# Linear attention on one core: the store of head 29 split 5, 121 and 2 and issued by GpSimd and SP, in place of 51, 13 and 64 by SP

## The chip, the core and the metric

The kernel runs on one core of one Trainium2 chip. The metric is the device time of one execution in microseconds (us). Three runs of the kernel before took 169.27, 169.34 and 169.89 us, median 169.34 us.

## What is computed

For each of 32 heads, with q, k and v of 2048 rows by 128 columns in bf16:

```python
phi_q = jnp.where(q > 0, q + 1, jnp.exp(q)) + 1e-6
phi_k = jnp.where(k > 0, k + 1, jnp.exp(k)) + 1e-6
kv = jnp.einsum("bhsd,bhse->bhde", phi_k, v)
z = jnp.einsum("bhsd->bhd", phi_k)
num = jnp.einsum("bhqd,bhde->bhqe", phi_q, kv)
den = jnp.einsum("bhqd,bhd->bhq", phi_q, z)[..., None] + 1e-6
return num / den
```

So each head reads three tensors of 512 KB and writes one of 512 KB: 50.33 MB in, 16.78 MB out.

## The kernel before

A head is one 128-partition tile per tensor: partition p holds 16 consecutive rows, 4096 bytes that are contiguous in the DRAM tensor too (`rows`). k, v and q each have six input buffers (`NBI`), the output `o_sb` has ten (`NBO`), and head h uses output buffer h mod 10. ScalarE takes the exponentials, GpSimd and VectorE make the clamped parts of phi, TensorE transposes q, sums phi_k times v into `kvz_ps` and then the numerators and denominators into `o_ps`, and VectorE (in the last heads ScalarE as well, `div_act`) divides into `o_sb`.

The order of the work is written out by hand. `Plan.add` registers an operation with its engine and a key; every engine, SP too, works its operations off in the order of their keys. `Plan.emit` adds the semaphore waits that the reads and writes call for. A DMA increments the semaphore of its slot by 16 (`dma=("o", slot)`), and a slot's semaphore is one of `dsems`. After its last DMA, SP waits until every slot of the output has its full count (the lines after `if e == "sp"`, line 226 of the profile); then the program ends.

All loads are issued by SP. The key of a store is `late = h + 1.0 + 0.18 * h`, which is later than the key of any load for the heads from 20 on, so the last dozen stores are issued after the last load. Heads 0 to 28 and 30 go out as one DMA of 128 partitions. Head 29 (`LAST - 2`) goes out as three DMAs by the tuple in `PARTS`: partitions 0 to 50, 51 to 63 and 64 to 127, all in slot 9. Head 31 goes out as two, tiles 0 to 8 (2304 bytes a partition) in slot 1 and tiles 9 to 15 (1792 bytes) in slot 10. No later head reuses the output buffer of heads 22 to 31.

GpSimd's own last operation is the addition of line 407 for head 31, with a key of 31.5; the key of the store of head 29 is 35.22.

Of the kernel before, what the change touches and what calls it, by code (L numbers as in the profile page):

```python
# [7 lines left out]
P = 128  # L8
# [241 lines left out]
def bass_standalone__linear_attn_elu__prompt_kernel(  # L250
# [6 lines left out]
    B, H, S, D = q.shape  # L257
    assert D == P and S == 16 * P
    NT = 16
# [3 lines left out]
    NBI = 6  # L263
    NBO = 10
# [2 lines left out]
    NG = 7  # L267
    HALF = NT * P // 2
    LAST = NH - 1
    PARTS = {LAST - 2: (51, 13, 64)}  # L270

    ADD = (1, 2, 3, 4, 5)
    SPLIT = tuple(j for j in range(NT) if j not in ADD)
# [8 lines left out]
    of = out.rearrange("b h s d -> (b h) s d")  # L282

    with ExitStack() as es:
# [28 lines left out]
        def dma_sem(name):  # L313
            return dsems[name]

        for n, c in (("k", NBI), ("q", NBI), ("v", NBI), ("va", 1), ("o", NBO + 1)):
            for i in range(c):
                dsems[(n, i)] = es.enter_context(nc.semaphore(f"s_{n}{i}"))

        block = es.enter_context(nc.Block())  # L320
        pl = Plan()

        def rows(x, h):
            return x[h].rearrange("(p j) d -> p (j d)", j=NT)
# [52 lines left out]
        for h in range(NH):  # L377
# [3 lines left out]
            bi, b2, b3, bo = h % NBI, h % 2, h % 3, h % NBO  # L381
# [201 lines left out]
                last_tile(h + 0.925)  # L583
                div(4, 5, h + 0.93)

            def store(t0, t1, key, parts, slot, p0=0, p1=P, h=h, bo=bo):
                pl.add("sp", key, lambda sp: sp.dma_start(rows(of, h)[p0:p1, t0 * D:t1 * D],
                                                          o_sb[p0:p1, bo, t0:t1].rearrange("p j d -> p (j d)")),
                       reads=[("o", bo, p) for p in parts], dma=("o", slot))

            late = h + 1.0 + 0.18 * h
            if h < LAST:
                p0 = 0
                for n in PARTS.get(h, (P,)):
                    store(0, NT, late, ("t", 0, 1, 2, 3, 4), bo, p0, p0 + n)
                    p0 += n
                assert p0 == P
            else:
                store(0, 9, late, (0, 1, 2), bo)
                store(9, NT, late + 0.01, (3, 4, "t"), NBO)  # L600
# [30 lines left out]
```

## Time and profile before

| | |
|---|---|
| median of three runs | 169.34 us |
| the profiled execution's own time | 169.59 us |
| its span, first to last instruction | 167.78 us |
| TensorE clock granted, mean | 0.991 |
| PE, DVE, ACT, POOL busy | 94%, 92%, 93%, 60% of the span |
| DMA | 67.25 MB, mean 401 GB/s |
| DMA, busy share of its 16 queues, 150 to 158 us | 1.02 to 1.03 (a full queue reads a little over 1) |

How to read it: times in the tables are counted from the first instruction. 1.81 us of the profiled execution lie outside the span. An issue by SP shows as a short instruction on SP's queue; when the data landed is read from the updates of the DMA's semaphore, of which the trace has one for each of the sixteen DMA queues that took part. The trace also has every DMA packet with its start, duration and size, but not the queue's number; since the packets of a busy queue follow each other within 4 ns, the packets can be strung into sixteen chains all the same. The last packet of a queue's share of a DMA is one of 4 bytes, which carries the semaphore's update.

### The profile page before, as it was taken

To read this page: it belongs to the slowest core of one execution; us is meant where nothing else is said; L and a number is where in the kernel's file an instruction comes from. 1 tells how busy PE (TensorE), PEld (TensorE's weight loads), DVE (VectorE), ACT (ScalarE), POOL (GpSimd) and SP (SyncE) were. 2 spreads that over 40 slices of the span, in tenths; PEclk is the share of its full clock that TensorE was granted. 3 is DMA by queue.
4 is the path that set the end of the run, shared out by engine and by line. 5 is a ranking of instruction groups with operands and counts; after the bars stand their busy time and mean duration, and the time that the engine had idled before them with its cause. 6 is when DMAs were issued, how large, how long until landed. Compare 5 with 4: busy or idle time off the path is not lost.

```text
span 167.8 us, 6512 instructions
## 1 busy us (share of the span) xinstructions
PE 158.3 (94%) x3143; PEld 151.3 (90%) x2449; DVE 154.2 (92%) x302; ACT 156.0 (93%) x143; POOL 100.8 (60%) x69
## 2 busy tenths in 40 slices
PE   7579999999999999999999999999999999999960
PEld 0259999999999999999999999999999999999950
DVE  0479999999999999999999999999999999999991
ACT  3969999999999999999999999999999999998790
POOL 2405677666666776666677766666777666666300
PEclk9999999999999999999999999999999999999996
DMA  5999999999999999999999999999999999999975
GB/s 192 367 419 421 413 410 416 413 421 408 414 417 416 419 418 417 421 419 416 414 419 421 415 417 422 416 417 420 418 419 419 420 415 417 421 418 415 410 242 221
DMA packets 19885, 67.25 MB, mean 401 GB/s; under 512 B 2082, under 2 KB 2210, under 8 KB 19874
## 3 DMA queue, kind: packets, MB, share of 16 engines
q1 hardware_dynamic: 19872, 67.12, 99.4%
q8 instruction: 5, 0.08, 0.2%
q14 instruction: 6, 0.05, 0.1%
q10 hardware_dynamic: 2, 0.00, 0.0%
HBM read 50.33 MB, written 16.78 MB: 400 GB/s over the span
## 4 chain that ended last, share of the span: by engine, by line
PE 85%; DVE 5%; DMA 4%; ACT 1%; SPq 1%; issue 0%; DVEq 0%
PE kvz_ps L428 35%; PE o_ps L499 17%; PE o_ps L500 16%; PE xT_ps L452 15%; DMA k_sb<-in_k_dram 4%; DVE o_sb L540 3%; PE kvz_ps L346 1%; ACT ek_sb L396 1%; SPq L389 1%; DVE rden_sb L528 1%; DVE rq_sb L472 0%; DVE emq_sb L484 0%; DVE den_sb L522 0%; DVE emk_sb L402 0%; DVE o_sb L533 0%
## 5 line engine op out<-in xcount | busy, mean ns | idle before, releaser
L407 POOL TENSOR_TENSOR rk_sb<-rk_sb,emk_sb 128x640 bf16<-128x640 bf16 x30 | 41.9, 1397 | 45.8 <-DVE emq_sb L484 44.5
L428 PE MATMUL kvz_ps<-v_sb,rk_sb 128*128 128x128 bf16 (+1 forms) x512 | 68.0, 218 | 0.9 <-DVE rk_sb L407 0.9
L540 DVE TENSOR_TENSOR o_sb<-o_ps,rden_sb 128x768 bf16<-128x768 f32 (+2 forms) x62 | 67.8, 1134 | 0.0
L399 POOL TENSOR_SCALAR rk_sb<-k_sb 128x2048 bf16<-128x2048 bf16 x31 | 58.7, 1895 | 9.5 <-DMA k_sb<-in_k_dram 9.5
L396 ACT ACTIVATE ek_sb<-k_sb 128x2048 bf16<-128x2048 bf16 x32 | 61.5, 1921 | 3.0 <-DMA k_sb<-in_k_dram 2.9
L463 ACT ACTIVATE eq_sb<-xT_ps 128x2048 bf16<-128x2048 bf16 (+1 forms) x33 | 60.1, 1825 | 3.3 <-PE xT_ps L452 2.2
L500 PE MATMUL o_ps<-kvs_sb,rq_sb 128*128 128x129 bf16 (+1 forms) x536 | 61.1, 217 | 0.0
L499 PE MATMUL o_ps<-kvs_sb,emq_sb 128*128 128x129 bf16 (+1 forms) x536 | 61.1, 217 | 0.0
L346 PE MATMUL kvz_ps<-ones_sb,rk_sb 128*128 128x1 bf16 x428 | 58.5, 165 | 0.0
L428 PE MATMUL kvz_ps<-v_sb,emk_sb 128*128 128x128 bf16 (+1 forms) x334 | 53.9, 218 | 0.8 <-DVE emk_sb L402 0.7
L499 PEld LDWEIGHTS o_ps<-kvs_sb,emq_sb 128*128 128x128 bf16 x536 | 50.6, 98 | 0.0
L500 PEld LDWEIGHTS o_ps<-kvs_sb,rq_sb 128*128 128x128 bf16 x536 | 50.1, 97 | 0.0
L428 PEld LDWEIGHTS kvz_ps<-v_sb,rk_sb 128*128 128x128 bf16 x512 | 46.4, 96 | 3.0 <-DVE rk_sb L407 1.8
L346 PE MATMUL kvz_ps<-ones_sb,emk_sb 128*128 128x1 bf16 x253 | 41.5, 165 | 0.0
L452 PE MATMUL xT_ps<-ident,q_sb 128*128 128x128 bf16 x512 | 33.8, 219 | 1.2 <-DMA q_sb<-in_q_dram 0.9
L452 PEld LDWEIGHTS xT_ps<-ident,q_sb 128*128 128x128 bf16 x512 | 29.9, 98 | 5.4 <-DMA q_sb<-in_q_dram 4.4
L428 PEld LDWEIGHTS kvz_ps<-v_sb,emk_sb 128*128 128x128 bf16 x334 | 32.1, 96 | 1.1 <-DVE emk_sb L402 0.8
L470 ACT ACTIVATE rq_sb<-xT_ps 128x1024 bf16<-128x1024 bf16 x30 | 30.5, 1018 | 0.0
L402 DVE TENSOR_SCALAR emk_sb<-ek_sb 128x2048 bf16<-128x2048 bf16 x32 | 21.9, 683 | 5.2 <-ACT ek_sb L396 5.2
L472 DVE TENSOR_SCALAR rq_sb<-xT_ps 128x1024 bf16<-128x1024 bf16 x34 | 23.3, 690 | 0.6 <-ACT eq_sb L463 0.6
L484 DVE TENSOR_SCALAR emq_sb<-eq_sb 128x2048 bf16<-128x2048 bf16 x32 | 22.0, 688 | 0.0
L533 DVE TENSOR_TENSOR o_sb<-o_ps,rden_sb 128x128 bf16<-128x128 f32 x31 | 9.0, 291 | 1.1
(29 smaller groups left out, 52.2 us busy)
## 6 DMA issues: line engine op xcount, KB each, us to landing
k_sb<-in_k_dram SPq DMA_DIRECT2D x32, 512.0 KB, 14.4
q_sb<-in_q_dram SPq DMA_DIRECT2D x32, 512.0 KB, 14.1
v_sb<-in_v_dram SPq DMA_DIRECT2D x32, 512.0 KB, 14.4
out_dram<-o_sb SPq DMA_DIRECT2D x30, 512.0 KB, 15.1
out_dram<-o_sb SPq DMA_DIRECT2D x1, 288.0 KB, 3.2
out_dram<-o_sb SPq DMA_DIRECT2D x1, 256.0 KB
out_dram<-o_sb SPq DMA_DIRECT2D x1, 224.0 KB, 3.1
out_dram<-o_sb SPq DMA_DIRECT2D x1, 204.0 KB
```

What stands on the lines that cost most here:

```text
L346: return pe.add_instruction(mybir.InstMatmult(start_tensor_calc=start, stop_tensor_calc=stop, ldweights=False, bass_skip_group_check=True, ...
L396: lambda a, bi=bi, b2=b2: a.activation(ek_sb[:, b2, :], k_sb[:, bi, :], ACT.Exp),
L399: lambda e, bi=bi, b3=b3: e.tensor_scalar(rk_sb[:, b3, :], k_sb[:, bi, :], BIG, 0.0, op0=ALU.min, op1=ALU.max),
L407: pl.add(eng, key, lambda e: e.tensor_tensor(out=rk_sb[:, b3, c], in0=rk_sb[:, b3, c], in1=emk_sb[:, b3, c], op=ALU.add), reads=[("emk", b ...
L428: last = pe.matmul(kvz_ps[:, 1 - l:NC + r], lhsT=w, rhs=v_sb[:, bi, c - l:c + D + r], start=first, stop=fin, skip_group_check=True)
L452: last = pe.transpose(xT_ps[:, j * P:(j + 1) * P], q_sb[:, bi, j * P:(j + 1) * P], ident[:])
L463: halves[part] = pl.add("act", key, lambda a: a.activation(eq_sb[:, b2, c], xT_ps[:, c], ACT.Exp), reads=both[part:part + 1] or both, writ ...
L470: f = lambda a: a.activation(rq_sb[:, b3, c], xT_ps[:, c], ACT.Relu)
L472: f = lambda d: d.tensor_scalar(rq_sb[:, b3, c], xT_ps[:, c], 0.0, None, op0=ALU.max)
L499: pe.matmul(o_ap, lhsT=emq_sb[:, b3, t * P:(t + 1) * P], rhs=kvs_sb[:, b3, c0:c1], start=True, stop=False)
L500: return pe.matmul(o_ap, lhsT=rq_sb[:, b3, t * P:(t + 1) * P], rhs=kvs_sb[:, b3, c0:c1], start=False, stop=True)
L540: pl.add("dve", key, lambda d: d.tensor_tensor(out=o_sb[:, bo, 3 * g0:3 * g1, :].rearrange("p (a b) d -> p a b d", b=3), in0=_ap(full, bas ...
```

## The change

The tuple for head 29 now names for each part the issuing engine, the slot and the number of partitions: GpSimd issues partitions 0 to 4 in a slot 11 of its own, then partitions 5 to 125 in a slot 12; SP issues partitions 126 and 127 in slot 9. Two semaphores are added. Nothing else differs: the same bytes go to the same places, and all other heads go out as before. The keys of the three parts are the same 35.22 as before, now on GpSimd's list and on SP's.

```diff
-    PARTS = {LAST - 2: (51, 13, 64)}
+    PARTS = {LAST - 2: (("pool", NBO + 1, 5), ("pool", NBO + 2, 121), ("sp", NBO - 1, 2))}
...
-        for n, c in (("k", NBI), ("q", NBI), ("v", NBI), ("va", 1), ("o", NBO + 1)):
+        for n, c in (("k", NBI), ("q", NBI), ("v", NBI), ("va", 1), ("o", NBO + 3)):
...
-            def store(t0, t1, key, parts, slot, p0=0, p1=P, h=h, bo=bo):
-                pl.add("sp", key, lambda sp: sp.dma_start(rows(of, h)[p0:p1, t0 * D:t1 * D],
+            def store(t0, t1, key, parts, slot, p0=0, p1=P, eng="sp", h=h, bo=bo):
+                pl.add(eng, key, lambda e: e.dma_start(rows(of, h)[p0:p1, t0 * D:t1 * D],
                                                           o_sb[p0:p1, bo, t0:t1].rearrange("p j d -> p (j d)")),
...
-                for n in PARTS.get(h, (P,)):
-                    store(0, NT, late, ("t", 0, 1, 2, 3, 4), bo, p0, p0 + n)
+                for eng, slot, n in PARTS.get(h, (("sp", bo, P),)):
+                    store(0, NT, late, ("t", 0, 1, 2, 3, 4), slot, p0, p0 + n, eng)
```

## The prediction, made before the result was known

> **What bounds the kernel now.** I read the last ten microseconds first, in the stretch table by 1 us: columns are the stretch, its length, busy time of PE, PE's weight loads, DVE, ACT and POOL, the granted clock, the DMA's busy share and GB/s.
>
> ```profile
> 162.00:163.00 1.00, 0.40 (x7) 0.22 (x4) 0.93 (x5) 0.86 (x4) 0.00 (x0) 1.00 0.31 107
> 163.00:164.00 1.00, 0.00 (x0) 0.00 (x0) 1.00 (x4) 0.97 (x4) 0.00 (x0) 1.00 0.98 393
> 164.00:165.00 1.00, 0.00 (x0) 0.00 (x0) 0.15 (x1) 0.00 (x0) 0.00 (x0) 0.80 0.92 360
> 165.00:166.00 1.00, 0.00 (x0) 0.00 (x0) 0.00 (x0) 0.00 (x0) 0.00 (x0) 0.50 0.85 328
> 166.00:167.00 1.00, 0.00 (x0) 0.00 (x0) 0.00 (x0) 0.00 (x0) 0.00 (x0) 0.50 0.19 71
> ```
>
> After 164.2 us no engine computes; only DMA is left, and in the last full microsecond just a fifth of its queues. So some queues end later than the rest. SP's waits after 156 us say the same (total, times, longest): line 226 is its closing wait.
>
> ```profile
> SPq L587 <- DVE o_sb L540: 4.5, 1, 4.5
> ...
> SPq L226 <- DMA out_dram<-o_sb: 2.5, 1, 2.5
> ```
>
> Then the issues: the timeline of the last division and of the last store (start, duration).
>
> ```profile
> 163.61 0.55 DVE L540 TENSOR_TENSOR o_sb<-o_ps,rden_sb 128x384 bf16<-128x384 f32 x1
> 164.18 0.33 SPq L587 DMA_DIRECT2D out_dram<-o_sb  x1
> ```
>
> Issued at 164.18, that store lands on its first queue at 166.10, on eleven queues by 166.25, and on the others at 166.63, 166.73, 167.00, 167.14 and **167.30**, the end. The program closes at 167.78, 0.48 us later.
>
> Which queues are those? Landing records of the late stores, in us; "late" are the last five of sixteen:
>
> ```
> head 28 (issued 153.54): 159.43 to 159.89 on 7 queues, 160.75 to 161.74 on 8, then 163.99
> head 30 (issued 162.13): 164.65 to 164.79 on 11; late 165.31 165.44 165.73 165.85 166.04
> head 31a (163.52):       165.50 to 165.66 on 11; late 166.05 166.17 166.43 166.59 166.75
> head 31b (164.18):       166.10 to 166.25 on 11; late 166.63 166.73 167.00 167.14 167.30
> ```
>
> One queue is over two microseconds behind after head 28; call it S. It falls behind on stores only: between loads its distance to the others stays (3.00 to 3.03 us behind the first for three loads near 130 us), with each store it grows by about 0.13 us. Stringing the packets into chains gives its path to the end: head 28 done at 163.47, one packet of 4 KB to 163.63, four more to 164.27, which lands at 164.76; eight of head 30 land at 166.04, then head 31 at 166.75 and 167.30. S never idles here. Its eight packets for head 30 took 166.04 - 164.76 = 1.28 us, **0.16 us a packet**. Three other chains take 17 packets, one and four of head 29 (ends 163.86, 164.14 and 164.28), so three of the five late queues are those on which the part of 51 was put; why the fifth ends at 166.63 I could not see.
>
> The trace thus shows how SP's parts were dealt: 51 as 17 packets on 3 queues, 13 as one on 13, 64 as four on 16; 32 landings, as the records have. S holds 1 + 4 = **5 packets** of head 29, is one of the thirteen, and is not one of the three.
>
> **The change part by part.**
>
> *SP's three issues go, one of 2 partitions stays.* They lasted 0.33, 0.32 and 0.94 us from 158.36 to 160.03; SP is next needed at 162.13. The cover is over 2 us, worth nothing either way. SP's closing list gets two waits more; the profile's take about 0.07 us for a pair, and they are passed while SP stands in the 2.5 us wait. Nothing.
>
> *GpSimd gets two issues and one wait.* Its last work:
>
> ```profile
> 155.42 1.40 POOL L407 TENSOR_TENSOR rk_sb<-rk_sb,emk_sb 128x640 bf16<-128x640 bf16 x1 [1.49 <-DVE emq_sb L484]
> ```
>
> From 156.82 POOL is idle. It will wait, as SP did, for DVE's division of head 29, which ended at 158.33. Behind that wait stand only its two DMAs and its end; nobody waits for them but SP's closing. An issue by POOL is in no row. Nearest are SP's: 0.32 us at the least, 3.01 us at the longest of line 587, and 163.00 - 162.13 = 0.87 us from issue to first packet. So the 121 partitions start moving between 158.36 + 2 x 0.32 + 0.87 = 159.9 and 158.36 + 2 x 3.01 + 0.87 = 165.3; nearest to an SP issue without a full queue, 160 to 161. This hardly matters for the end: S is busy until 166.0 without head 29, so its packets cost their own length whenever they come before that, and the other queues, done at 165.8, have slack to S of over a microsecond. A start decides only from about 166 on, 7.6 us after release.
>
> *The share of S.* The end is 167.30 + 0.16 x (packets of head 29 on S, less 5). Bounds: none, -0.80 us; all that can be, one of 5, one of 2 and eleven of 121, +1.28 us (dealt as SP deals, 121 = 11 x 11 goes on 11 queues). The nearest row is the whole store: 121 of 128 partitions, and each 128-partition store in the trace puts eight packets on every queue. I take eight, and for the 5 and the 2 none on S, since 2 and 5 reach at most seven of sixteen queues. 8 - 5 = 3, times 0.16 = **+0.48 us**. What goes from the three queues with 22 packets brings nothing, as they ended before S.
>
> The Trainium skill, "DMA: Bandwidth & Descriptors", section "Why a DMA increments its semaphore by 16 and not by 1", says that a DMA uses the most queues up to 16 that divide its outer count (the rows of 51, 13 and 64 agree), on GpSimd from a moving start; it also reports an exception in which GpSimd's plain copies are dealt over all sixteen, rounded up, which would be 8 on fifteen queues and 1 on the last. By the exception the sum is the +0.48 us above; the plain rule gives rival 2 or 3. No run so far shows which holds.
>
> **Sum.** 169.59 + 0.48 = 170.07 us for the profiled execution. That one lies 0.25 us over the median of 169.34; on the median's footing the forecast is 169.34 + 0.48 = **169.8 us**.
>
> **Rivals.**
>
> 1. *S is spared (faster).* If the part of 121 is dealt over 11 queues and S is among the other five, S holds one packet or none: 4 x 0.16 = -0.64 us, 168.7 us; with none -0.80, 168.5. The next late end would be the unexplained 166.63, so at most 0.67 us are gained, unless that one goes too; then the floor is 166.25. For it: 121 divides by 11, and SP's parts were dealt by division. Against: eleven of sixteen queues take the big part. It decides as soon as S gets fewer than five.
>
> 2. *S is among the eleven (slower).* Eleven packets on S: 6 x 0.16 = +0.96 us, 170.3 us. The same dealing; eleven queues of sixteen make it about twice as likely as rival 1, whose five must hold S.
>
> 3. *The way by GpSimd has its own price (slower).* Packets that follow one another take 0.159 us in most rows, but 0.29 to 0.31 us while queues restart at 161 us. Were S's eight 0.30 each, that is 2.40 - 0.80 = +1.60 us, 170.9 us. The Trainium skill, same page, section "Latency and other measured facts", holds two of the sixteen queues to be usually slower and guesses at descriptors made by GpSimd. Here one queue lags with no DMA by GpSimd in the program, so that cannot be all of it. A cost of GpSimd's DMA at the program's close, now 0.48 us, would act alike.
>
> 4. *The change does not do what it says*, or S is another queue in other executions: 169.3 us.
>
> **How the numbers follow.** Forecast, with S at eight or nine packets: 0.40 (+0.48 to +0.64 us). Spared: 0.13. Among eleven: 0.23. Own price: 0.19. No effect: 0.05. The range reaches from the spared case, 168.6, to 170.7, leaving out most of the own-price case above it. A difference of 0.5%, 0.85 us, is about what a measurement of this kernel can tell from no change. Faster by more than that needs the spared case with the fifth late queue gone: 0.06. Within: the forecast, the rest of the spared case, no effect and some of the edges: 0.51. Slower by more: the cases 2 and 3 with few exceptions, and the forecast if its packets run a little long: 0.43.
>
> **What would show it.** In the profile after: the number of packets of head 29 on the last chain (8 expected; 1 and 11 are the rivals); the last landing near 167.8; SP's closing wait up from 2.5 to about 3.0 us; no compute instruction at another time, the last division ending at 164.16 as before; the three chains with 22 packets gone, so that the landings of the last store fall in one group of fifteen and one straggler. Packets of head 29 clearly longer than 0.16 us would mean rival 3. Wrong altogether would be a last landing that is not on S, or a POOL start after 166.

## The result, and the profile after

The kernel after takes **169.90 us** (median of 12 runs, 169.78 to 170.17), the kernel before in the same comparison 169.34 us (median of 12, 169.18 to 170.09). The ratio is **1.003, 95% interval 1.0021 to 1.004**: 0.56 us slower, where 169.8 us and +0.48 us were forecast. The profiled execution has a span of 168.17 us, 0.39 us over that of before.

The first view is the stretch table of the kernel after, with the same columns as in the prediction.

```profile
164.00:165.00 1.00, 0.00 (x0) 0.00 (x0) 0.31 (x1) 0.14 (x1) 0.00 (x0) 0.86 0.92 364
165.00:166.00 1.00, 0.00 (x0) 0.00 (x0) 0.00 (x0) 0.00 (x0) 0.00 (x0) 0.50 0.92 354
166.00:167.00 1.00, 0.00 (x0) 0.00 (x0) 0.00 (x0) 0.00 (x0) 0.00 (x0) 0.50 0.13 51
167.00:168.00 1.00, 0.00 (x0) 0.00 (x0) 0.00 (x0) 0.00 (x0) 0.00 (x0) 0.50 0.01 5
```

Most queues now finish together: the DMA is still at 0.92 between 165 and 166 us, where it was at 0.85. But a thinner tail reaches further: 0.13 in place of 0.19 between 166 and 167, and 5 GB/s after 167, where the kernel before has nothing:

```profile
167.00:168.00 1.00, 0.00 (x0) 0.00 (x0) 0.00 (x0) 0.00 (x0) 0.00 (x0) 0.50 0.00 0
```

The store was evened out over most queues and made the last queue later.

SP's waits after 156 us (total, times, longest):

```profile
SPq L226 <- DMA out_dram<-o_sb: 2.7, 2, 2.3
```

In the timeline of the kernel after, VectorE's last division (start, duration):

```profile
163.76 0.55 DVE L540 TENSOR_TENSOR o_sb<-o_ps,rden_sb 128x384 bf16<-128x384 f32 x1
```

And GpSimd's two issues, which the timeline puts together:

```profile
158.80 1.67 POOL L587 DMA_DIRECT2D out_dram<-o_sb  x2 [1.83 <-DVE o_sb L540]
```

SP's closing wait is 2.7 us, not the 3.0 forecast, since the compute of this execution ran 0.15 us later (the last division ends at 164.31, before at 164.16), and the end moved by 0.39 us between the two profiled executions in place of 0.48. GpSimd's two issues lasted 0.71 and 0.96 us; its first packet moved at 160.08, the part of 5 landed first at 160.40 and the part of 121 at 162.07. The view of the DMA queues shows the new one:

```profile
q1 hardware_dynamic: 19716, 66.60, 98.0%
q0 software_dynamic: 176, 0.52, 1.0%
```

The 176 packets of q0 are 126 of 4096 bytes (one for each partition), 32 that update semaphores, and 18 more of 4 bytes that stand for nothing. These 18 tell the dealing. If a part is dealt over all sixteen queues with the share rounded up, the part of 5 has one packet on five queues and 16 - 5 = 11 empty places, the part of 121 has eight on fifteen and one on the last, 16 x 8 - 121 = 7 empty places: 18.

Strung into a chain as before, S runs like this: among its packets of head 28 stands one of the part of 5; then **eight packets of q0** from 163.40 to 164.67 without a gap; then head 30 to 165.93 and head 31 to 167.23, which lands at **167.69**, the end. S has nine packets of head 29, one more than forecast. The landings of the last store (issued at 164.34) are 166.22 to 166.39 on thirteen queues and 166.71, 167.07 and 167.69 on the others.

A measure that leaves out when the compute ran: from the last landing of head 27 to the end, both on S. Before it is 167.30 - 162.69 = 4.61 us, after 167.69 - 162.40 = 5.29 us, +0.68 us; four packets of 0.16 us are 0.64 us. This measure, "the stretch of S", is used below.

### The profile page after: what moved, and what is told of

It reads as the page before. It is cut to its first block, busy times and chain, and to the rows that moved or that the text cites. A ratio compares the mean times of both kernels' runs of the same rounds, so it can differ in the third digit from the quotient of the medians.

```text
span 168.2 us, 6513 instructions
## 1 busy us (share of the span) xinstructions
PE 158.4 (94%) x3143; PEld 151.4 (90%) x2449; DVE 154.3 (92%) x302; ACT 155.9 (93%) x143; POOL 102.5 (61%) x71
## 4 chain that ended last, share of the span: by engine, by line
PE 85%; DVE 5%; DMA 4%; ACT 1%; SPq 1%; issue 0%; DVEq 0%
PE kvz_ps L428 35%; PE o_ps L499 17%; PE o_ps L500 16%; PE xT_ps L452 15%; DMA k_sb<-in_k_dram 4%; DVE o_sb L540 3%; PE kvz_ps L346 1%; ACT ek_sb L396 1%; SPq L389 1%; DVE rden_sb L528 1%; DVE rq_sb L472 0%; DVE emq_sb L484 0%; DVE den_sb L522 0%; DVE emk_sb L402 0%; DVE kvs_sb L445 0%
```

## The experiments

Each kernel is the changed one with another tuple in `PARTS`, unless more is shown. Ratios are to the kernel before on the same chip in the same comparison. On some chips the times of the kernel before stand in two groups (17 of 29 at 169.2 to 169.6 us and 12 at 169.9 to 170.9 in the comparison of `sp_128`), which makes some intervals wide; medians of one comparison are set against each other where that helps.

**Head 29 as one store by SP** (`sp_128`, and once more as `sp_128_again`): GpSimd and the split are out, S holds eight.

```diff
+    PARTS = {}
```

> Head 29 goes out as one store of 128 partitions by SP, like the other heads; GpSimd issues nothing. Theory (the share of the slow queue S): eight packets of head 29 on S in place of five before, 3 x 0.16 = +0.48 us against the kernel before, about 169.8 us, the same as the changed kernel. Rival (the way by GpSimd has a price of its own): without GpSimd's DMAs the time goes back to that of the kernel before, 169.3 us, or nearly.

> Head 29 as one store of 128 by SP once more, since its first comparison with the kernel before was wide. Eight packets on S: +0.48 us against the kernel before by the share of S, 0.16 us less than the changed kernel with nine; by the price of GpSimd's way no loss.

Measured: 169.73 us, ratio 0.9992 (0.9971 to 1.0013), and 169.71 us, ratio 1.0012 (0.9993 to 1.0032). The profiles show eight packets of head 29 on S and stretches of 5.08 and 5.05 us, +0.47 and +0.44 to the 4.61 of before: three packets, as forecast. In the medians it is smaller, +0.14 and +0.30 us. Both intervals include no change, and the first ends at +0.22 us, short of the +0.48 us forecast. The count is confirmed in the traces and the size in time is not.

**5, 121 and 2, all by SP** (`sp_5_121_2`): the same parts without GpSimd.

```diff
+    PARTS = {LAST - 2: (("sp", NBO - 1, 5), ("sp", NBO - 1, 121), ("sp", NBO - 1, 2))}
```

> The same three parts as the changed kernel, all issued by SP. SP dealt 51 over 3 queues and 13 over 13, so 121 = 11 x 11 should go over 11 queues with eleven packets each. Theory (share of S): if S is among the eleven, 11 packets, 6 x 0.16 = +0.96 us, 170.3 us (12 packets and 170.5 if S takes one of the 5 too); if S is not among them, 0 packets and 168.5 to 168.7 us. Rival (price of GpSimd's way): 169.3 us.

Measured: 170.48 us, ratio 1.0048 (1.0021 to 1.0074). SP deals 121 as eleven packets on eleven queues, S among them: its chain has eleven packets in a row from 163.53 to 165.25, after one of the part of 5. The stretch is 5.76 us (+1.15). The same parts cost more by SP (+0.89 us in the median, +1.15 in the stretch) than by GpSimd in the kernel after (+0.56 and +0.68): what differs is the dealing, not the price of a packet.

**51, 13 and 64, all by GpSimd** (`pool_51_13_64`): the split of before, issued by GpSimd.

```diff
+    PARTS = {LAST - 2: (("pool", NBO + 1, 51), ("pool", NBO + 2, 13), ("pool", NBO + 2, 64))}
```

> The parts of the kernel before, all three issued by GpSimd. Theory (share of S) with GpSimd dealing over all sixteen queues rounded up: 51 as four on 13 queues, 13 as one on 13, 64 as four on 16, so S, if among the first thirteen, holds 9 packets: 4 x 0.16 = +0.64 us, 170.0 us. Were GpSimd to deal by division as SP does: 5 packets, 169.3 us. Rival (price of GpSimd's way alone): 0.5 us or, with three issues in place of two, some more, 169.9 to 170.2 us; it is told apart by the packets counted on S.

Measured: 170.07 us, ratio 1.0024 (0.9998 to 1.005, which just includes no change), the stretch 5.27 us (+0.66).

```profile
q0 software_dynamic: 192, 0.52, 1.1%
```

Of these 192 packets 128 have 4096 bytes and 48 update semaphores, so 16 stand for nothing: 16 x 4 - 51 = 13 and 16 - 13 = 3. So 51 goes as four on S and not on three queues as SP deals it, and S holds 4 + 1 + 4 = 9. This is the dealing rounded up once more.

**Which queue is S** (`which_queue`): SP issues 56 partitions and then 12, 11, 10 and so on down to 4; a part of n puts one packet on the first n queues, so S shows its place by how many it gets.

```diff
+    PARTS = {LAST - 2: (("sp", NBO - 1, 56),) + tuple(("sp", NBO - 1, n) for n in (12, 11, 10, 9, 8, 7, 6, 5, 4))}
```

> Head 29 in ten parts by SP: 56, 12, 11, 10, 9, 8, 7, 6, 5 and 4 partitions. 56 goes as four packets on 14 queues; a part of n from 12 to 4 as one packet on the first n queues. The number of packets of head 29 on S tells its place: 4 + 9 if it is the fourth queue, one less for each place further, 4 if it is the thirteenth. Theory (share of S): the time goes with that number at 0.16 us a packet against five before; S as the eighth queue would hold 4 + 5 = 9, +0.64 us, and SP's ten issues of some 0.33 us end just before it is next needed. Rival (S is not a fixed queue, or the parts are not dealt from the first queue on): a number outside 4 to 13.

Measured: 170.56 us in a single run. After its four packets of the 56, S takes 1.90 us less the 0.63 of those four, which is eight singles of 0.16: those of 12 down to 5. S is the **fifth queue** in the order of dealing. A part of 5 always reaches it.

**The kernel after once more, and its count without GpSimd** (`after_again`, `sp_112_11_5`): SP alone, 112 as seven on sixteen, 11 and 5 as one each, S holds nine.

```diff
+    PARTS = {LAST - 2: (("sp", NBO - 1, 112), ("sp", NBO - 1, 11), ("sp", NBO - 1, 5))}
```

> The changed kernel once more, beside the next three. By the runs so far S is the fifth queue, so it takes one packet of the part of 5 and eight of the part of 121: nine against five before. Theory (share of S): 4 x 0.16 = +0.64 us against the kernel before, 170.0 us. Rival (a price of GpSimd's way on top of the share): more than the same share by SP.

> Head 29 by SP alone in parts of 112, 11 and 5: seven packets on each of 16 queues, one on the first eleven, one on the first five, so nine packets on S as in the changed kernel, without GpSimd. Theory (share of S): the same time as the changed kernel, +0.64 us against the kernel before. Rival (a price of GpSimd's way): less than the changed kernel by that price, at the least 169.3 us.

Measured: 169.85 us, ratio 1.0029 (1.0018 to 1.004) for the kernel after, and 170.01 us, ratio 1.0035 (1.0022 to 1.0049) for the same count by SP; stretches 5.25 and 5.22 us. No GpSimd, the same loss.

**GpSimd with the count of before** (`pool_with_5`): SP issues 51, GpSimd 13 and 64. Rounded up these are one on thirteen and four on sixteen, so S holds five.

```diff
+    PARTS = {LAST - 2: (("sp", NBO - 1, 51), ("pool", NBO + 1, 13), ("pool", NBO + 2, 64))}
```

> The parts of the kernel before, with the 51 by SP and 13 and 64 by GpSimd; GpSimd deals these as SP does, so S holds 1 + 4 = 5 packets as before, all of them by way of GpSimd. Theory (share of S): no difference from the kernel before. Rival (a price of GpSimd's way): slower, by 0.5 us if the whole of the change's loss is that price.

Measured: 169.42 us, before 169.41, ratio **0.9998** (0.9985 to 1.0012); the stretch 4.56 us. GpSimd with two issues and two semaphores more, without the count: no difference. This and the run before it separate the two theories.

**Four packets fewer on every queue** (`drop_64`): the part of 64 is not stored, so partitions 64 to 127 of head 29 stay unwritten.

```diff
+    PARTS = {LAST - 2: (("sp", NBO - 1, 51), ("sp", NBO - 1, 13))}
...
-                assert p0 == P
+                assert p0 == sum(x[2] for x in PARTS.get(h, (("", 0, P),)))
```

> The part of 64 of the kernel before is left out (partitions 64 to 127 of head 29 are not written), the parts of 51 and 13 stay, so S holds one packet of head 29 and every other queue four less. Theory (share of S): 4 x 0.16 = -0.64 us, 168.7 us, S still last. Rival (something other than S ends the program): less gain, none if the end hangs on the issue and latency of the last store.

Measured: 168.75 us, ratio 0.997 (0.9955 to 0.9985), 0.66 us less than its 169.41 of before; four packets of 0.16 are 0.64. S has one packet between heads 28 and 30 and still lands last, 0.42 us after the next queue. Three rows of its stretch table show how short the tail becomes:

```profile
164.00:165.00 1.00, 0.00 (x0) 0.00 (x0) 0.00 (x0) 0.00 (x0) 0.00 (x0) 0.53 0.99 381
165.00:166.00 1.00, 0.00 (x0) 0.00 (x0) 0.00 (x0) 0.00 (x0) 0.00 (x0) 0.50 0.30 115
166.00:167.00 1.00, 0.00 (x0) 0.00 (x0) 0.00 (x0) 0.00 (x0) 0.00 (x0) 0.50 0.00 0
```

**One packet fewer on S, sixteen more on another queue** (`sp_68_60`): SP deals 68 as 17 on four queues and 60 as four on fifteen. S holds four. The first four queues hold 21, where before the first three held 22 and the fourth five.

```diff
+    PARTS = {LAST - 2: (("sp", NBO - 1, 68), ("sp", NBO - 1, 60))}
```

> Head 29 by SP in parts of 68 (4 x 17: seventeen packets on each of the first four queues) and 60 (four on each of the first fifteen). S as the fifth queue holds four packets, one less than before, the four first queues 21 in place of 22 and 5. Theory (share of S): -0.16 us, at the edge of what can be measured, 169.2 us. Rival (the first queues with 21 packets become the last): no gain or a loss.

Measured: 170.10 us, ratio 1.0037 (1.0015 to 1.0059). The gain did not come. The chain that ends last has 17 and then 4 packets of head 29, so it is one of the first four queues; presumably the fourth, since the other three had 22 packets before and ended by 167.14. That chain is done with head 28 at 161.92 and lands the end at 168.08. The chain of S, followed on from its head 28, has four packets of head 29 and lands at 166.70, 4.44 us after its head 27. That fits one packet fewer (4.61 - 0.16 = 4.45), but S no longer sets the end. So S is the bound only as long as no other queue is given more than its lead, and the lead is not the same for all of them.

**5 and 121 by GpSimd, each partition as two halves** (`pool_halves`): the same bytes; source and target of GpSimd's parts count the two halves of 2048 bytes, the second first, in a dimension of their own.

```diff
+                def two(x):
+                    if eng == "sp":
+                        return x
+                    n = (t1 - t0) * D // 2
+                    return bass.AP(x.tensor, x.offset + n, [list(x.ap[0]), [-n, 2], [1, n]])
-                pl.add(eng, key, lambda e: e.dma_start(rows(of, h)[p0:p1, t0 * D:t1 * D],
+                pl.add(eng, key, lambda e: e.dma_start(two(rows(of, h)[p0:p1, t0 * D:t1 * D]),
```

> The changed kernel, with GpSimd's two parts written as two halves of 2048 bytes in each partition, the second half first, so that the DMAs count in a second dimension (twice the packets, half the size). The question is how GpSimd deals these. Theory (share of S, whatever the form): the time follows from the bytes on S. Dealt rounded up over sixteen queues as in the changed kernel: the bytes of nine packets of 4 KB, +0.64 us against the kernel before, 170.0 us. Dealt by division from the first queue on, 5 on the first five and 121 on the other eleven: S, the fifth queue, holds one, -0.64 us, 168.7 us, unless the next late queues end it sooner. Dealt by division with S among the eleven: eleven, +0.96 us, 170.3 us. Rival (the smaller packets or the second dimension cost by themselves): slower than the count of bytes says.

Measured: 169.17 us, ratio 0.998 (0.9954 to 1.0005).

```profile
q1 hardware_dynamic: 19716, 66.60, 98.4%
q0 software_dynamic: 224, 0.52, 1.1%
```

Of 224 packets, 126 have 4096 bytes again, 32 update semaphores, and **66** of 8 bytes stand for nothing: 11 for the part of 5 and 5 x 11 = 55 for the part of 121. So these parts were dealt by division: 5 on five queues, 121 as eleven on the eleven others. S has one packet, as in rival 1 of the prediction. The median falls by 0.24 us, in an interval that includes no change (-0.78 to +0.08 us), and not by 0.64: in the last store (issued at 164.08) four queues land from 165.98 to 166.10 and twelve between 166.39 and 166.96. Now the eleven are late, with S or without it.

**Both evened out** (`spared`): the same form with 5 and 99 by GpSimd, and six stores of 4 by SP.

```diff
+    PARTS = {LAST - 2: (("pool", NBO + 1, 5), ("pool", NBO + 2, 99)) + 6 * (("sp", NBO - 1, 4),)}
```

> Head 29 by GpSimd as 5 and 99 partitions, each partition written as two halves of 2048 bytes, which in the run of the halves made the dealing go by division (5 on five queues, S among them, and the rest on the eleven others), and six SP stores of 4 partitions, one packet on each of the first four queues. S gets one packet, the eleven get nine each in place of eleven, the first four seven each. If the end is set by the queue that is furthest behind: S alone would give -0.64 us; the halves ended on the eleven queues at about -0.24 us, and two packets fewer there are worth 0.31 us more, about -0.55 us: 168.8 to 168.9 us, a ratio near 0.9965. Rival: what held the halves at -0.24 us was not the count on the eleven queues but GpSimd's late start or its own price; then the time stays at that of the halves, a ratio of 0.998 to 1.0.

Measured: **168.77 us** (168.62 to 169.05), before 169.52 in this comparison, ratio **0.9952** (0.9935 to 0.997). This is faster than both kernels. The end of its stretch table and its queues:

```profile
164.00:165.00 1.00, 0.00 (x0) 0.00 (x0) 0.00 (x0) 0.00 (x0) 0.00 (x0) 1.00 0.98 384
165.00:166.00 1.00, 0.00 (x0) 0.00 (x0) 0.00 (x0) 0.00 (x0) 0.00 (x0) 1.00 0.39 151
166.00:167.00 1.00, 0.00 (x0) 0.00 (x0) 0.00 (x0) 0.00 (x0) 0.00 (x0) 1.00 0.00 0
```

```profile
q1 hardware_dynamic: 19760, 66.69, 99.0%
q0 software_dynamic: 192, 0.43, 0.8%
```

The 192 are 104 of 4096 bytes, 32 updates, and 11 + 5 x 9 = 56 of 8 bytes that stand for nothing, so the dealing is as meant. The stretch of S is 4.05 us. One of the first four queues ends its last packet a little later than S (165.96 against 165.93); that S still lands last is inferred from its slower landings in the other runs (see the open ends below), and by the other order its stretch would be 3.95 us. Fourteen queues land the last store within 0.22 us, and two follow 0.70 and 0.80 us after the first; before, the last came 1.20 us after the first.

All counts together, the stretch of S in each profiled execution beside the median's distance to the kernel before of the same comparison:

| packets of head 29 on S | kernels | stretch of S, us | median less before, us |
|---|---|---|---|
| 1 | `drop_64`, `spared` | 3.97, 4.05 | -0.66, -0.75 |
| 5 | before, `pool_with_5` | 4.61, 4.56 | 0, +0.01 |
| 8 | `sp_128`, again | 5.08, 5.05 | +0.14, +0.30 |
| 9 | after, again, `sp_112_11_5`, `pool_51_13_64` | 5.29, 5.25, 5.22, 5.27 | +0.56, +0.44, +0.60, +0.48 |
| 12 | `sp_5_121_2`, `which_queue` | 5.76, 5.73 | +0.89, a single run |

The stretches lie on one line, 4.0 us and 0.16 us for every packet over the first, within 0.08 us, by whichever engine the parts were issued. Each is from one profiled execution. In the medians the intervals of `sp_128` (both times) and `pool_51_13_64` include no change, so for these the size rests on the stretch.

## Why the prediction was right, point by point

*The bound.* S ends last and never idles: shown. With nine packets on S the last store was issued at 163.19 us in `sp_112_11_5` and at 164.34 us in the kernel after, and the stretches of these two differ by 0.07 us. Within these times it does not matter to S when the compute ends.

*SP's issues and GpSimd's.* Nothing, as forecast. GpSimd's issues lay within the bounds of 0.32 and 3.01 us that were taken from SP's, and its packets moved from 160.08, in the 160 to 161 that was chosen.

*The share of S.* The term was mis-sized by one packet. "For the 5 and the 2 none on S" failed: S is the fifth queue of the dealing order, and a part of 5 takes the first five; the 2 does not reach it. Eight for the 121 was right. So 9 - 5 = 4 packets and +0.64 us by the prediction's own price, where +0.48 was forecast; measured are +0.56 us (0.36 to 0.68 by the interval) in the medians and +0.68 us in the stretch. The forecast's case was "eight or nine packets", and the time fell into it. The eight itself was partly luck: its reason was the nearest row, a store of 128 by SP, while SP deals these 121 as eleven packets on S (`sp_5_121_2`); it came true because GpSimd deals plain rows in another way, which no run had shown then.

The trace agrees with the exception that the Trainium skill, "DMA: Bandwidth & Descriptors", section "Why a DMA increments its semaphore by 16 and not by 1", reports for some direct copies by GpSimd: 18 empty places here, and 16 in `pool_51_13_64`. For the same bytes with a second dimension the 66 empty places of `pool_halves` agree with the section's plain rule by division, and the eleven after the five with its moving start. The prediction lets the plain rule lead to "rival 2 or 3"; by its own list that is rival 1 or 2, S among the other five or among the eleven.

*Rival 1, S spared.* It did not happen in the change, but it can be made: `drop_64` gives its -0.64 us as -0.66. The prediction's floors for it, 166.63 and 166.25, were landings of other queues with their packets of before. They left out that eleven of these queues would hold eleven packets in place of four or five, and `pool_halves`, which is this case, ends on such queues at 166.96. *Rival 2, eleven on S*, is the dealing by SP. With the packet of the 5 it is twelve, for which the price of 0.16 us gives +1.12: the stretch measured +1.15, the median +0.89 (+0.36 to +1.25 by the interval). *Rival 3, a price of GpSimd's own*, is refuted by `pool_with_5` (0.9998) and by `sp_112_11_5`, which loses as much without GpSimd; in the chain the eight packets of q0 took 0.159 us each. *Rival 4* is out: the change did what it says, and in every profiled run the count on S fits the fifth queue in the order of dealing.

*The signs.* "One group of fifteen and one straggler" was wrong: thirteen and three. S is the last of the three, so it does not bear on the time; which the two others are, at 0.48 and 0.85 us after the first, I could not see. Other executions have one of them or none (`sp_128_again`), so they are not part of the change.

*What stays open.* Why S loses about 0.13 us on each store and none on loads: up to three of its eight packets of head 30 take 0.164 to 0.176 us where the rest take 0.159 to 0.162, but no run varied what could cause that. S is late in a second way: from its last packet to its landing it takes 0.43 to 0.46 us in the runs that end on it, while the queues on which the other two runs end take 0.34 (`sp_68_60`) and 0.35 us (`pool_halves`). The cause of that is open too. And why the median with eight packets lies at +0.14 and +0.30 us while its stretches give +0.46. Between the fastest executions (12 of each, against 29 of the kernel before) it is +0.31 and +0.46 us, so the two groups of times, which raise the median of the kernel before, are probably a part of it. Each program also has five instruction fetches of 16 KB (the queue q8 of the page), whose packets take 0.90 to 1.08 us each, between 15 and 46 us; one of them falling on S might move the end. That is argued, not shown.

## What to carry to other kernels

Where DMA is full to the end, do not ask how many bytes or issues move, but how many packets fall on the queue that ends last: string the packets into chains, count, and price one packet from the same chain. The number of partitions in a part and the engine that issues it decide which queues get how many. In the counts tried here SP used as many queues as the largest divisor up to sixteen, the first ones, and GpSimd rounded up over sixteen, or divided where a second dimension was counted. A store late enough to be cut up is a means to level the queues, as `spared` shows with 0.5%, but whatever is taken from the slowest must not land on a queue that has less lead than it gets.

## What the runs showed of the hardware

One DMA queue of sixteen, in the run that could tell it (`which_queue`) the fifth in SP's order of dealing, lags in every profiled execution here, without any DMA by GpSimd in the program too: head 28 lands last 4.56 us after its first landing before, 4.31 us in `sp_128`. GpSimd's DMAs cost as much per packet as SP's here, 0.159 us, and two of them in place of SP's left the time as it was (0.9998, 0.9985 to 1.0012). The same copy by GpSimd is dealt in two ways by the form in which its bytes are counted: 18 packets that carry nothing for plain rows, 66 for rows in two halves. The last landing of the lagging queue comes 0.43 to 0.46 us after its last packet, that of other queues 0.34 us (`sp_68_60`) and 0.35 us (`pool_halves`).
